# One load of a weight's first 10 KB for 128 partitions becomes loads of 5, 5, 5, 1 and 112 partitions

## The chip, the cores and the metric

The program runs on one core of a Trainium2 chip. The core has TensorE (PE, with its weight loads as PEld), VectorE (DVE), ScalarE (ACT), GpSimd (POOL) and SyncE (SP), and 16 DMA engines that move data between HBM and the on-chip memory SBUF, which has 128 partitions. The metric is the device time of one execution in microseconds; three runs are timed and the median counts. A profile of one further execution shows where the time lies.

## The reference

It is a decode step of attention with a KV cache, gated by a small MLP. All data are float32.

```
x: (2, 1, 512)   k_cache, v_cache: (2, 32, 8192, 128)   wq: (512, 4096)   wo: (4096, 512)
w1: (512, 1376)  b1: (1376)  w2: (1376, 512)  b2: (512)

xn = layernorm(x)
q  = (xn @ wq) split into 32 heads of 128
p  = softmax(q . k_cache / sqrt(128))          # one query row per head, 8192 keys
o  = p . v_cache                               # joined to (2, 1, 4096)
s  = o @ wo
g  = silu(gelu(layernorm(xn) @ w1 + b1) @ w2 + b2)
out = x + s * g
```

The caches are 537 MB together and are read once; wo is 8 MB and is read at the end.

## The kernel before

Two heads form a unit, so there are N = 32 units. Of a unit, K is 8 MB: half a head's keys stand in 64 partitions, 64 KB to a partition. Two buffers hold K in turn, a third, `big[2]`, holds V. For each unit VectorE multiplies K with the query row and sums over the 128 columns, TensorE and ScalarE do the softmax, and TensorE forms the product of the weights and V. The loops of the engines run beside each other and are tied by semaphores that are taken down again (`take`).

All big loads are issued by SP on one queue, in the order in which the code stands: w1, wq, the first K, w2, the second K, two small loads of x into `x4` (lines 299 to 301, 4 partitions with 512 B each), then V and K in turn (lines 305 to 320). ScalarE's queue carries three small loads at the very start: x (2 partitions), b1 and b2 (1 partition each; lines 199 to 201). The last V (unit 31) goes in two halves into a K buffer, so that `big[2]` is free for wo before the last unit is done.

wo is laid out as `(p c) n -> p c n`: partition p holds rows 32p to 32p+31, that is 32 pieces of 512 numbers, 64 KB. It comes in seven pieces after `p_free`, cut at c = 0, 10, 18, 24, 28, 30, 31, 32 (`WO_CUTS`, line 90), the last of them in two halves of columns (`LAST_COLS`, line 91); semaphore `d_wo0` stands for the first piece, up to `d_wo6` and `d_wol` (lines 323 to 325). The pieces shrink, so that little is left to do when the last one lands.

At the end TensorE multiplies the normalised output `on` with wo, c by c (lines 526 to 543). The first 28 go in four row groups of one bank (`pw`), ScalarE copies it (`wide`, line 378), the last four go into `acc`, and the copy is added. VectorE applies the gate and adds x (lines 379 to 381), SP stores (line 382) and waits for the store.

Each DMA raises its semaphore by 16 once it has all landed; TensorE's matmuls of a piece wait for 16 on that piece's semaphore.

## Time and profile before

| | |
|---|---|
| median of three runs | 1300.62 us (1300.08 to 1300.69) |
| the profiled execution | 1299.61 us |
| its span, first to last instruction | 1298.3 us |
| HBM read | 559.30 MB, 431 GB/s over the span |
| VectorE busy | 1135.7 us (87%) |
| TensorE busy | 460.9 us (35%) |
| ScalarE busy | 72.0 us (6%) |
| first issue of wo | 1266.90 us |
| end of TensorE's last matmul | 1295.79 us |

The span is shorter than the time of the execution by 1.31 us, which lie before the first and after the last instruction. Times in the rows are microseconds from the start of the span. The profile does not name the DMA engine that carried a packet. How many engines are at work can be read from the DMA share of a short stretch (a share of 1.00 is all 16), and how many have ended a load from the 4-byte packets, one of which closes an engine's part of a load and raises the semaphore.

### The profile page before, as it was taken

What the parts mean: (1) busy time and instruction counts of PE and PEld (TensorE: products, weight loads), DVE (VectorE), ACT (ScalarE), POOL (GpSimd) and SP (SyncE); (2) the same over time, 40 slices, a digit from 0 to 9 for tenths busy, and PEclk for the clock granted to TensorE, in tenths of its full rate; (3) what the DMA queues carried; (4) which work ended last, traced back from release to release, by engine and by line L of the source; (5) the groups of instructions that cost most, each with busy time, mean ns of one, the idle gap of its engine ahead of it and who ended that gap; (6) DMA issues with size and microseconds to landing.
All of it is one profiled execution on the core that took longest, in us unless ns stands there. A gap on an engine that the chain in (4) does not pass through costs nothing. (4 is left out here: it accounts for less than half of the span.)

```text
span 1298.3 us, 7389 instructions
## 1 busy us (share of the span) xinstructions
PE 460.9 (35%) x2958; PEld 148.7 (11%) x2958; DVE 1135.7 (87%) x171; ACT 72.0 (6%) x245; POOL 2.1 (0%) x14
## 2 busy tenths in 40 slices
PE   3813433322433322343322334322334321343337
PEld 1201111001111000111100111100111100111103
DVE  2599999988889988889988888988888988888991
ACT  1100000000000000000000000000000000000000
POOL 0000000000000000000000000000000000000000
PEclk8756776567677556777656777656776666677659
DMA  9999999999999999999999999999999999999998
GB/s 410 436 428 442 430 432 432 428 444 428 438 430 428 440 428 444 428 434 430 428 444 428 440 430 426 440 428 444 428 434 430 430 442 428 440 430 430 423 436 361
DMA packets 11242, 559.39 MB, mean 431 GB/s; under 512 B 1264, under 2 KB 1536, under 8 KB 1892
## 3 DMA queue, kind: packets, MB, share of 16 engines
q1 hardware_dynamic: 11228, 559.30, 99.7%
q8 instruction: 4, 0.07, 0.0%
q10 hardware_dynamic: 8, 0.01, 0.0%
q14 instruction: 2, 0.02, 0.0%
HBM read 559.30 MB, written 0.00 MB: 431 GB/s over the span
## 5 line engine op out<-in xcount | busy, mean ns | idle before, releaser
L51 DVE TENSOR_TENSOR big<-big,Q 128x16384 f32<-128x16384 f32 (+1 forms) x33 | 551.3, 16707 | 73.2 <-DVEq L45 73.2
L51 DVE TENSOR_REDUCE sc<-big 128x128 f32<-128x16384 f32 (+1 forms) x33 | 551.2, 16703 | 4.8
L51 PE MATMUL bank<-big,PZ 128*8 128x512 f32 x2048 | 291.1, 732 | 628.9 <-PEq L45 628.9
L51 PEld LDWEIGHTS bank<-big,PZ 128*8 128x8 f32 x2048 | 60.1, 103 | 832.6 <-issue 832.6
L51 PE MATMUL bank<-Q,ident 128*128 128x512 f32 (+2 forms) x198 | 78.5, 506 | 0.2 <-issue 0.2
L51 ACT COPY o<-bank 128x512 f32<-128x512 f32 x33 | 19.4, 586 | 891.6 <-ACTq L45 880.0
L51 PE MATMUL bank<-ident,MX 128*1 128x128 f32 x32 | 9.3, 291 | 137.9 <-PEq L45 137.8
L51 PE MATMUL bank<-mod,o 128*128 128x2 f32 x256 | 32.8, 250 | 27.4 <-PEq L45 27.4
L51 PEld LDWEIGHTS bank<-mod,o 128*128 128x128 f32 x256 | 31.0, 191 | 55.4 <-issue 55.4
L51 PEld LDWEIGHTS bank<-Q,ident 128*128 128x128 f32 x198 | 33.6, 198 | 16.5 <-issue 16.5
L51 ACT ACTIVATE PZ<-sc,bias 64x128 f32<-64x128 f32 x64 | 25.5, 399 | 6.6 <-ACTq L45 6.2
L51 DVE TENSOR_REDUCE nm<-bank 1x2 f32<-1x128 f32 x32 | 8.9, 279 | 18.9 <-DVEq L45 18.9
L51 DVE TENSOR_TENSOR big<-big,mine 64x512 f32<-64x512 f32 (+1 forms) x2 | 4.5, 2279 | 21.6 <-ACT big L51 21.6
L51 PEld LDWEIGHTS bank<-ident,MX 128*1 128x1 f32 x32 | 2.5, 79 | 162.9 <-issue 162.9
L51 ACT COPY bias<-bank 128x1 f32<-128x1 f32 x32 | 5.1, 159 | 225.2 <-ACTq L45 225.2
L51 PE MATMUL bank<-nm,srow 1*64 1x1 f32 x128 | 10.4, 219 | 10.0 <-PEq L45 9.4
L51 PE MATMUL bank<-big,sides 64*128 64x512 f32 x16 | 12.6, 958 | 3.7 <-DVE big L51 3.7
L51 DVE TENSOR_REDUCE MX<-sc 128x1 f32<-128x128 f32 x32 | 9.2, 286 | 4.7
L51 PE MATMUL bank<-big,xnT 128*2 128x512 f32 x64 | 9.3, 748 | 10.3 <-DMA big<-in_A_wq_dram 10.3
L51 ACT ACTIVATION_READ_ACCUMULATOR PZ<-sc,bias x64 | 11.8, 184 | 0.0
L51 DVE SCALAR_TENSOR_TENSOR res<-bank,gate 128x128 f32<-128x128 f32 x1 | 0.3, 292 | 12.1 <-PE bank L51 12.1
L51 PEld LDWEIGHTS bank<-nm,srow 1*64 1x64 f32 x128 | 8.6, 165 | 16.2 <-issue 16.2
(78 smaller groups left out, 74.8 us busy)
## 6 DMA issues: line engine op xcount, KB each, us to landing
big<-in_A_k_cache_dram SPq DMA_DIRECT2D x2, 4096.0 KB, 35.9
big<-in_A_v_cache_dram SPq DMA_DIRECT2D x2, 4096.0 KB, 35.9
big<-in_B_w_dram SPq DMA_DIRECT2D x1, 2752.0 KB, 10.2
big<-in_B_w_dram SPq DMA_DIRECT2D x1, 2560.0 KB, 52.1
big<-in_A_wo_dram SPq DMA_DIRECT2D x1, 2560.0 KB, 14.7
big<-in_A_wo_dram SPq DMA_DIRECT2D x1, 2048.0 KB, 19.3
big<-in_A_wo_dram SPq DMA_DIRECT2D x1, 1536.0 KB, 22.5
big<-in_A_wo_dram SPq DMA_DIRECT2D x1, 1024.0 KB, 24.5
```

Of the source, the lines that this page charges most:

```text
L51: ins = getattr(self.engines[eng], method)(*args, **kwargs)
```

## The change

The first piece of wo, c = 0 to 9 (20 KB in each partition), was one load. Its first half, c = 0 to 4 (`FEW` = 5, 10 KB in each partition), is now issued for partitions 0 to 4, 5 to 9, 10 to 14, 15 and 16 to 127 apart, in this order (`SHARES`), and its second half, c = 5 to 9, for all partitions in one load. All six loads raise `d_wo0`, so the matmuls of that piece wait for 6 x 16 = 96. The other pieces are as before.

```diff
@@ -89,6 +89,8 @@
     LAST_COLS = (0, D // 2, D)
+    FEW = 5
+    SHARES = (0, 5, 10, 15, 16, P)
@@ -320,7 +322,9 @@
     wo_v = wo.rearrange("(p c) n -> p c n", p=P)
-    for i, (c0, c1) in enumerate(zip(WO_CUTS, WO_CUTS[1:])):
+    for a0, a1 in zip(SHARES, SHARES[1:]):
+        op("SP", "dma_start", wo_sb[a0:a1, :FEW, :], wo_v[a0:a1, :FEW, :], sig="d_wo0")
+    for i, (c0, c1) in enumerate(zip((FEW,) + WO_CUTS[1:], WO_CUTS[1:])):
         for h, (n0, n1) in enumerate(zip(LAST_COLS, LAST_COLS[1:]) if c1 == OC else [(0, D)]):
@@ -525,7 +529,7 @@
-            after = [t["on"], t["mem"], (f"d_wo{i}", 16)]
+            after = [t["on"], t["mem"], (f"d_wo{i}", 16 * (len(SHARES) if i == 0 else 1))]
```

On SP, after the last two halves of V, the program's order at the loads of wo changes as follows (`big` is the buffer that wo shares with V; partitions x numbers):

```order
 L51 DMA big<-in_A_v_cache_dram 128x8192 x2
-L51 DMA big<-in_A_wo_dram 128x5120
+L51 DMA big<-in_A_wo_dram 5x2560 x3
+L51 DMA big<-in_A_wo_dram 1x2560
+L51 DMA big<-in_A_wo_dram 112x2560
+L51 DMA big<-in_A_wo_dram 128x2560
 L51 DMA big<-in_A_wo_dram 128x4096
 L51 DMA big<-in_A_wo_dram 128x3072
```

One load has become six; those behind it keep their order. On the other engines no instruction moves.

## Rows read from the trace of the kernel before

**Rows 1.** Page, parts 1 to 3: busy time, DMA share in 40 slices, packets
```profile
PE 460.9 (35%) x2958; PEld 148.7 (11%) x2958; DVE 1135.7 (87%) x171; ACT 72.0 (6%) x245; POOL 2.1 (0%) x14
...
DMA  9999999999999999999999999999999999999998
...
DMA packets 11242, 559.39 MB, mean 431 GB/s; under 512 B 1264, under 2 KB 1536, under 8 KB 1892
```

**Rows 2.** Chain that ended last, in order of time: start, length, what
```profile
1268.70 25.32 DMA big<-in_A_wo_dram
...
1294.06 1.73 PE bank L51 x40
...
1295.82 0.30 DVE res L51
```

**Rows 3.** Timeline, 1266 to 1296 us: start, length, engine, operation, idle before
```profile
1266.90 3.65 SPq L51 DMA_DIRECT2D big<-in_A_wo_dram  x8
...
1283.85 0.21 PEld L51 LDWEIGHTS bank<-big,on 128*17 128x17 f32 x8 [0.27 <-issue]
...
1292.77 0.20 PEld L51 LDWEIGHTS bank<-big,on 128*17 128x17 f32 x8 [1.48 <-DMA big<-in_A_wo_dram]
...
1295.35 0.15 PEld L51 LDWEIGHTS bank<-big,on 128*17 128x17 f32 x4 [0.17 <-DMA big<-in_A_wo_dram]
```

**Rows 4.** DMA issues: what, count, size, microseconds from issue to landing
```profile
big<-in_A_wo_dram SPq DMA_DIRECT2D x1, 2560.0 KB, 14.7
```

**Rows 5.** Stretches near the end: length, GpSimd, clock, DMA share, GB/s
```profile
1293.00:1293.20 0.20, 0.00 (x0) 1.00 1.03 369
...
1293.80:1294.40 0.60, 0.00 (x0) 1.00 0.34 121
```

**Rows 6.** Packets begun in 1273.39:1273.40 (with share), 1274.86:1275.12, 1274.91:1274.93, 1275.09:1275.12
```profile
q1 hardware_dynamic: 1, 0.00, 5.6%
...
DMA packets 13, 0.16 MB, mean 630 GB/s; under 512 B 5, under 2 KB 5, under 8 KB 5
...
DMA packets 4, 0.06 MB, mean 3072 GB/s; under 512 B 1, under 2 KB 1, under 8 KB 1
...
DMA packets 2, 0.02 MB, mean 683 GB/s; under 512 B 1, under 2 KB 1, under 8 KB 1
```

**Rows 7.** Packets begun in 73.45:73.85, 73.85:73.95 and 74.80:75.20, second K and x4
```profile
DMA packets 28, 0.53 MB, mean 1319 GB/s; under 512 B 14, under 2 KB 20, under 8 KB 20
...
DMA packets 6, 0.07 MB, mean 666 GB/s; under 512 B 3, under 2 KB 5, under 8 KB 5
...
DMA packets 8, 0.26 MB, mean 655 GB/s; under 512 B 4, under 2 KB 4, under 8 KB 4
```

**Rows 8.** ScalarE's queue: packets in 1.60:1.77 (x) and 2.75:2.76 (b1)
```profile
DMA packets 2, 0.00 MB, mean 24 GB/s; under 512 B 0, under 2 KB 0, under 8 KB 2
...
q10 hardware_dynamic: 1, 0.01, 131.9%
```

**Rows 9.** Packets begun in 1195.8:1196.36, 1196.36:1196.40 and 1197.3:1197.6
```profile
DMA packets 16, 0.52 MB, mean 936 GB/s; under 512 B 8, under 2 KB 8, under 8 KB 8
...
DMA packets 2, 0.07 MB, mean 1638 GB/s; under 512 B 1, under 2 KB 1, under 8 KB 1
...
DMA packets 8, 0.26 MB, mean 874 GB/s; under 512 B 4, under 2 KB 4, under 8 KB 4
```

**Rows 10.** Instruction queue: packets, MB, share, in 148.4:149 and 1203.60:1204.0
```profile
q14 instruction: 1, 0.01, 3.2%
...
q14 instruction: 1, 0.01, 5.1%
```

**Rows 11.** Packets begun in 1215.69:1215.79, 1216.65:1216.90 and 1216.69:1216.71
```profile
DMA packets 0, 0.00 MB, mean 0 GB/s; under 512 B 0, under 2 KB 0, under 8 KB 0
...
DMA packets 13, 0.26 MB, mean 1049 GB/s; under 512 B 5, under 2 KB 5, under 8 KB 5
...
DMA packets 2, 0.03 MB, mean 1639 GB/s; under 512 B 1, under 2 KB 1, under 8 KB 1
```

## The prediction

> **What bounds the kernel now.** Begin with the page's slices: the share of the 16 DMA engines stands at 9 tenths from the second slice to the last but one, 431 GB/s on average; VectorE, the busiest of the others, has 87% of the span [rows 1]. The kernel is bound by its loads, and each DMA engine moves 431 / 16 = 26.9 GB/s, so 10 KB of one partition (10,240 B, called a row below) cost an engine 0.38 us. Then read the chain of waits from its end: the last things on it are the wait for a piece of wo, 1.73 us of TensorE, and vector work at 1295.82 [rows 2]. The timeline of that stretch says the same from the other side: TensorE is already waiting when the later pieces arrive, 1.48 us before the fourth and 0.17 us before the last half piece [rows 3]. So whatever moves the last landing of wo moves the end by as much, 1 to 1. The first piece is different. It lands 14.7 us after its issue at 1266.90, at 1281.6, and TensorE asks for it only once the normalised attention output is there, at 1283.85 [rows 3, 4]: 2.2 us of room.

> The next view is the one that decides. Over the last microseconds the DMA share falls in steps: all engines work at 1293.0, and from 1293.8 to 1294.4 the share is 0.34, which is 5.4 of 16 [rows 5]. Eleven engines are done and five still have their last pieces to move. They are not slower, they are late: where the last load of v ends, the earliest engine writes its closing 4-byte packet at 1273.39, and five do so from 1274.86 to 1275.12, the last at about 1275.10, which is 1.71 us behind the first [rows 6]. Since all have the same bytes of wo from there on, that distance is still there at the end. An end-of-kernel gain is to be had by taking bytes from those five and from no others.

> **The change part by part.** Before, every engine carries 8 of the 128 partitions in every load. Now the first 10 KB go out as 5 + 5 + 5 + 1 rows and 112 rows. The 112 give each engine 7 rows. A load with few rows uses few engines, as the trace has it: the two 4-row loads of x late in the setup put their eight 512 B packets on engines that are among the nine earliest of the load ahead of them, none on the last four [rows 7], two packets to an engine, and the 2-row and 1-row loads of the biases and x on the other queue are 2 packets and 1 packet [rows 8]. So I take five engines, the same each time and including the four of the 4-row loads, to get one row from each 5-row load, and the first of them the single row too:
> - eleven engines: 7 rows instead of 8, -1 x 0.38 = -0.38 us;
> - four receivers: 7 + 3 = 10, +2 x 0.38 = +0.76 us;
> - the first receiver: 7 + 3 + 1 = 11, +3 x 0.38 = +1.14 us.

> [...] The 5.4 KB row of b1 left in one packet [rows 8], so the measurement decides for one engine. [...]

> So the question is whether a receiver is one of the five late ones. In the setup none of the four known receivers is: the last four engines of that load have no 512 B packet. But the latest of the four is the ninth in order: eight engines end before 73.85, then comes one that has both a 512 B pair and its own closing packet from 73.85 to 73.95 [rows 7]. An engine starts its next packet as the last one ends, so its place can be followed from load to load. I followed this one up to 1196: it is again the ninth, with eight ahead of it and four far behind, closing between 1196.36 and 1196.40 [rows 9] (meanwhile one early engine fell back, and one that stood behind has come ahead, slowly, by drift). At 1203.6 an 8 KB instruction packet of another queue arrives on one engine [rows 10]; a packet of the same kind at 148 is the one after which the early engine fell back [rows 10]. At the end of the next load the ninth place, 1215.69 to 1215.79, is empty, and the late group has five members instead of four, the new one at 1216.69 to 1216.71 [rows 11]. It lost about 1 us. By this reading the fifth late engine is a receiver. At the end of v it closes at 1274.91 to 1274.93 [rows 6], so 1274.92 - 1273.39 = 1.53 us behind the first.

> The sum, as lags behind today's first engine: the late receiver 1.53 + 0.76 = 2.29; the late engines that give, at most 1.71 - 0.38 = 1.33; an early receiver, at most 0.45 + 1.14 = 1.59 (0.45 is an estimate: 0.40 is the width of the window in which the first eight close [rows 7], and 0.05 is for drift). The last landing moves by 2.29 - 1.71 = +0.58 us.

> The other parts. Each engine now has 15 or more packets where it had 8, plus one to six closing packets; a closing packet took 5.6% of 16 engines over 0.01 us, 0.009 us [rows 6]. The extra handling of eight packets is not shown; it lies between 0 and 8 x 0.009 = 0.07 us. I take 0.04, the middle. Issues: SP's eight wo issues took 3.65 us, 0.46 each [rows 3]; there are 13 now, so +2.3 us, the last issue at about 1272.9. The cover is the v load still in flight until 1273.39 at the earliest engine [rows 6]; the first wo issue is not later, so no engine runs dry. Without that cover it would cost at most 2.3 us. SP has nothing queued behind them but the store. TensorE's wait for the first piece now asks for six loads' count instead of one and is no new instruction; with +0.6 us the piece lands at 1282.2, and the 2.2 us of room hide it. The later waits shift with the landings. Sum: 0.58 + 0.04 = +0.62 us.

> The profiled execution took 1299.61 us, of which 1298.3 are the span. By its own time the changed kernel takes 1300.23. The median of the three runs is 1.01 us above it, so the forecast on their footing is 1300.62 + 0.62 = 1301.24 us.

> **The rivals.**
> 1. Relief. No receiver is late: the instruction packet at 1203.6 falls elsewhere or not at all in the timed executions, or I lost the thread of the ninth engine between 74 and 1196 us. Then the last is the late giver at 1.33 or the first receiver at up to 1.59, and the end moves by -0.38 to -0.12, with +0.04 for packets: about 1300.4 us. For it: in the setup the four are early [rows 7]. Against it: rows 9 to 11, and the fifth receiver is known by nothing here; four of the twelve other engines are late from the start, and if it is one of those the shift is again +0.5 to +0.8. [...]
> 2. One engine for five rows. If an odd count of rows isn't dealt out one to an engine, all 16 split rows fall on one: 7 + 16 = 23 rows, +15 x 0.38 = +5.7 us on it. If it is the earliest engine the end moves by 5.7 - 1.71 = +4.0, if the latest by +5.7: about 1305.4 us, slower. It decides from the point where that engine's surplus passes 1.71 us plus 2.6, some 12 rows. For it: no odd count other than 1 stands in the trace. Against it: 1, 2 and 4 rows went to as many engines.
> 3. The split loads are dealt over all engines in equal parts. Then every engine has its old bytes, nothing moves but the packets: 1300.66 us. Rows 7 and 8 speak against it.

> **How the numbers follow.** Forecast 0.64, relief 0.24, one engine 0.04, even dealing 0.05, something not seen 0.03. What this measurement can tell from no change is about 0.2%, 2.6 us. Forecast, relief and even dealing all lie within it; one engine and half of the unseen make slower, and the rest of the unseen is divided: faster 0.02, same 0.93, slower 0.05. The range runs from the best relief, 1300.62 - 0.38, less 0.3 for the scatter of the runs (0.6 us between lowest and highest), 1299.9, to a late first receiver, 1300.62 + 0.58 + 0.38 + 0.04, plus 0.4 for scatter, 1302.1.

> **What would show it.** In the new profile: more 10 KB packets, 1 row in 16 on few engines; the DMA share after the bulk of the wo pieces standing at 1 to 3 sixteenths where it stood at five, for about 1 us; the last wo landing some 0.6 us later behind the earliest engine than 1.7 us; SP's issues at about 6 us for 13. If the late group loses 0.38 us and nothing sticks out behind it, relief is right. If one engine works alone for 4 us, rival 2 is. If the share falls as before, rival 3. The instruction packet at 1203.6 missing or on another engine would break the step that I trust least.

## The result and the profile after

The changed kernel takes 1304.71 us (median of 10 runs, 1303.81 to 1305.63), the kernel before 1300.63 (10 runs). The ratio is 1.0031 with a 95% interval of 1.0021 to 1.0041: slower by 0.3%, 4.1 us, and above the range that was given (1299.9 to 1302.1). The profiled execution took 1304.4 us with a span of 1303.1, which is 4.8 us longer than the span before.

The page of the kernel after has the same lines of busy time to within 1 us, as many bytes, and a last slice that moves 297 GB/s where it had 361. These are its DMA share, its packets and its rate [answering rows 1]:

```profile
PE 461.6 (35%) x2958; PEld 149.6 (11%) x2958; DVE 1135.7 (87%) x171; ACT 71.9 (6%) x245; POOL 2.1 (0%) x14
...
DMA  9999999999999999999999999999999999999998
...
DMA packets 11401, 559.37 MB, mean 429 GB/s; under 512 B 1296, under 2 KB 1568, under 8 KB 1924
```

The chain that ended last, kernel after, has the same members as before in [rows 2], behind more issues of SP; the wait for wo is longer, and its end has moved from 1294.02 to 1298.80, by 4.8 us:

```profile
1270.60 28.20 DMA big<-in_A_wo_dram
...
1298.85 1.75 PE bank L51 x39
...
1300.62 0.30 DVE res L51
```

The timeline of the kernel after from 1266 to 1299 us answers rows 3. Two waits are new: TensorE waits for the second half of the last V, which was there before, and for the first piece of wo, which had 2.2 us of room:

```profile
1267.06 7.32 SPq L51 DMA_DIRECT2D big<-in_A_wo_dram  x13
...
1277.50 3.62 PE L51 MATMUL bank<-big,PZ 128*8 128x512 f32 x32 [0.89 <-DMA big<-in_A_v_cache_dram]
...
1286.49 0.19 PEld L51 LDWEIGHTS bank<-big,on 128*17 128x17 f32 x8 [1.86 <-DMA big<-in_A_wo_dram]
...
1297.59 0.19 PEld L51 LDWEIGHTS bank<-big,on 128*17 128x17 f32 x8 [1.49 <-DMA big<-in_A_wo_dram]
```

Where the time went is read from one view, stretches of the timeline with the DMA share and the rate (columns: stretch, length, GpSimd busy, granted clock, DMA share, GB/s). First the kernel before:

```profile
1268.00:1273.00 5.00, 0.00 (x0) 1.00 0.99 426
1273.00:1275.00 2.00, 0.00 (x0) 1.00 0.84 358
...
1283.00:1285.00 2.00, 0.00 (x0) 1.00 0.97 414
...
1273.00:1283.00 10.00, 0.00 (x0) 1.00 0.96 410
```

And the kernel after:

```profile
1268.00:1273.00 5.00, 0.00 (x0) 1.00 1.02 439
1273.00:1275.00 2.00, 0.00 (x0) 1.00 0.86 221
...
1283.00:1285.00 2.00, 0.00 (x0) 1.00 1.01 421
...
1273.00:1283.00 10.00, 0.00 (x0) 1.00 0.96 219
```

From 1273 to 1283 us the engines are busy to the same 0.96, and move 219 GB/s instead of 410. That is (410 - 219) x 10 us = 1.91 MB less, and at 431 GB/s it takes 4.4 us to make up for them. Before 1273 and after 1283 us the rates are about equal. So for ten microseconds the engines are slow together, and none is left working alone. The tail of the kernel after has the late engines again, up to some 7 of 16 where five stood in [rows 5], for little more than a microsecond:

```profile
1298.60:1299.00 0.40, 0.00 (x0) 1.00 0.46 161
1299.00:1299.60 0.60, 0.00 (x0) 1.00 0.16 56
```

So a DMA engine counts as busy also while its packet is held up: the share is 0.96 in both, at 410 and at 219 GB/s. The share says nothing of it; the rate at the same share does.

### The profile page after: what moved, and what is told of

The parts are those of the page before. It is cut to its first block, busy times and chain, and to the rows that moved or that the text cites. A ratio compares the mean times of both kernels' runs of the same rounds, so it can differ in the third digit from the quotient of the medians.

```text
span 1303.1 us, 7394 instructions
## 1 busy us (share of the span) xinstructions
PE 461.6 (35%) x2958; PEld 149.6 (11%) x2958; DVE 1135.7 (87%) x171; ACT 71.9 (6%) x245; POOL 2.1 (0%) x14
## 2 busy tenths in 40 slices
DMA packets 11401, 559.37 MB, mean 429 GB/s; under 512 B 1296, under 2 KB 1568, under 8 KB 1924
## 5 line engine op out<-in xcount | busy, mean ns | idle before, releaser
L51 PE MATMUL bank<-big,PZ 128*8 128x512 f32 x2048 | 288.2, 726 | 629.5 <-PEq L45 628.6
L51 PE MATMUL bank<-big,on 128*17 128x512 f32 (+1 forms) x88 | 11.8, 595 | 3.9 <-DMA big<-in_A_wo_dram 3.9
```

The costliest lines, as they stand in the source:

```text
L51: ins = getattr(self.engines[eng], method)(*args, **kwargs)
```

## The experiments

Three theories stood after the result. Places, an assumption that no trace had shown: a load of 128 partitions gives each DMA engine partitions of its own, and with other counts several engines write to the same part of SBUF and hold each other up. Size or source: 10 KB pieces, or their order in HBM, are read slowly. Surplus: what the prediction had, the fullest engine sets the end. Each run is compared with the kernel before on the same chip, which took 1299.9 to 1300.0 us there. The edits shown are those at the loads; where the number of loads changes, the count that TensorE (or SP) waits for changes with it. All are against the changed kernel, but for those where half of V is cut, which are against the kernel before.

**Two halves of 10 KB, no split by partitions.**

```diff
-    SHARES = (0, 5, 10, 15, 16, P)
+    SHARES = (0, P)
```

> The first 20 KB of wo come in two loads of 10 KB, each for all 128 partitions; nothing is split by partitions. Three theories. Places: the 4 us come from splitting by partitions (a load of 128 partitions gives each DMA engine a group of partitions of its own, other counts make engines meet); here nothing meets, so 1300.6 to 1300.8 us, and 10 KB packets take 0.38 us each. Size: pieces of 10 KB out of rows of 64 KB are read more slowly than pieces of 20 KB; all 256 pieces are there as in the changed kernel, so about 1304.7 us and packets of 0.6 to 1.0 us. Surplus: the end is set by the fullest engine; here all are equal, so 1300.6 us.

1300.04 us against 1300.03, ratio 0.9999 (0.9990 to 1.0009). The stretch as above:

```profile
1273.00:1283.00 10.00, 0.00 (x0) 1.00 0.95 400
```

10 KB pieces out of rows of 64 KB run at about the old rate (400 against 410 GB/s). The theory of size falls, and the second half of the change, c = 5 to 9 in one load, costs nothing.

**The few-row loads alone.** They bring their bytes a second time, into units of Q that no one reads any more.

```diff
+    for a0, a1 in ((0, 5), (5, 10), (10, 15), (15, 16)):
+        op("SP", "dma_start", Q[a0:a1, 4:24, :]..., wo_v[a0:a1, :FEW, :]..., sig="d_few")
-    SHARES = (0, 5, 10, 15, 16, P)
+    SHARES = (0, P)
```

> As with two loads of 10 KB for all partitions, and ahead of them loads of 5, 5, 5 and 1 partitions that bring the same bytes a second time, into a part of Q that is no longer read; SP also waits for them at the end. Places: five engines at a time write into partitions 0 to 15, where two to four engines have their own data, so these meet with the last load of v and with wo: 2 to 3.7 us by a count of engines that share a group (an estimate from the 0.38 us of a row), 1302.6 to 1304.3 us. Surplus: the receivers have 3 rows more, the first 4, so at most 1.53 + 1.14 - 1.71 = +1.0 us, 1301.0 to 1301.6 us. Size: 1304.7 us or more, as for the two halves alone.

1302.04 us, ratio 1.0015 (1.0006 to 1.0025): +2.0 us, at the lower end for places. It is above the +1.0 that surplus allows, but the interval, +0.8 to +3.2 us, still holds that. What surplus does not have is the loss of rate that these 160 KB bring to the stretch:

```profile
1273.00:1283.00 10.00, 0.00 (x0) 1.00 0.97 367
```

**The load of 112 partitions alone.** The loads of 5, 5, 5 and 1 are left out.

```diff
-    for a0, a1 in zip(SHARES, SHARES[1:]):
+    for a0, a1 in ((16, P),):
```

> The loads of 5, 5, 5 and 1 partitions are left out (the first 10 KB of partitions 0 to 15 are not brought, so the products of 80 rows of wo are not right); the load of 112 partitions and the second half stay. Places: the 112 rows, 7 to an engine, lie across the groups of 8, so most engines meet another one: +1.9 to +4.8 us by the same count, 1302.5 to 1305.4 us, and the packets of 10 KB take 0.6 us and more. Surplus: every engine has a row less, so -0.4 us, 1300.2 us. Size: 240 of the 256 pieces, about 1304.3 us.

1303.63 us, ratio 1.0029 (1.0018 to 1.0041). With fewer bytes and no surplus on any engine it loses 3.6 us by the medians:

```profile
1273.00:1283.00 10.00, 0.00 (x0) 1.00 0.96 269
```

So the larger part of the cost comes with the 112 rows and not with the five-row loads. The two parts together (2.0 + 3.6) are more than the 4.1 of the whole, but by no more than the intervals of these runs, so whether they overlap is not shown.

**16 and 112 partitions.**

```diff
-    SHARES = (0, 5, 10, 15, 16, P)
+    SHARES = (0, 16, P)
```

> The first 10 KB come in one load of 16 partitions and one of 112: 1 + 7 rows for every engine, no engine has more than before. Places: still 112 rows across the groups, and 16 engines meet in the first 16 partitions: +2.6 to +6.0 us, 1303.2 to 1306.6 us. Surplus: equal bytes on every engine, so 1300.6 to 1300.8 us. Size: 1304.7 us.

1304.98 us, ratio 1.0035 (1.0021 to 1.0050), +4.95 us by the medians. If 16 and 112 rows are dealt out in equal parts, all engines have the bytes they had before, and surplus cannot make this. Here, too, the rate is what is lost:

```profile
1273.00:1283.00 10.00, 0.00 (x0) 1.00 0.94 230
```

**Another source.** The same loads to the same partitions, read from 1.3 MB without gaps.

```diff
+    wo_f = wo[:FEW * P, :].rearrange("(p c) n -> p c n", p=P)
-        op("SP", "dma_start", wo_sb[a0:a1, :FEW, :], wo_v[a0:a1, :FEW, :], sig="d_wo0")
+        op("SP", "dma_start", wo_sb[a0:a1, :FEW, :], wo_f[a0:a1], sig="d_wo0")
```

> The same five loads into the same partitions as in the changed kernel, but the rows are read from another place: row p from byte 10240 p of wo on, so 1.3 MB without gaps and not 10 KB out of every 64 KB (the numbers are not those of wo's first piece, so the product is not right). If the places in SBUF make the cost, it stays: +3.5 to +5 us over before, 1303.5 to 1305 us, with GB/s of 170 to 280 for some 7 us after the last load of v. If the way of reading HBM makes it (the order or the gaps of the rows), it goes: 1300.0 to 1300.6 us.

1304.5 us, ratio 1.0040 (1.0026 to 1.0054): the cost stays, and so does the rate:

```profile
1273.00:1283.00 10.00, 0.00 (x0) 1.00 0.94 224
```

So neither the gaps nor the addresses in HBM make it (224 GB/s here, 219 with them).

**64 and 64 partitions.**

```diff
-    SHARES = (0, 5, 10, 15, 16, P)
+    SHARES = (0, 64, P)
```

> The first 10 KB come in two loads of 64 partitions, 4 rows to each of 16 engines in both, so every engine has 8 rows as before. [...] If what counts is only that a load uses all 16 engines with equal rows: 1300.0 to 1300.5 us. If any split by partitions costs as much as that of 112 rows: +3.6 us or more.

1304.99 us, ratio 1.0039 (1.0025 to 1.0054): +5.0 us. That a balanced split costs at all speaks for places, but by its time alone this run fits the last case of the expectation, that any split by partitions costs as much as that of 112 rows. At the half rate that the long loads of 64 in the next run show (203 to 216 against 416 GB/s), the 8 rows of an engine would take 2 x 8 x 0.38 = 6.1 us instead of 3.0, an estimate of about +3.0 us, and the measured cost is more. The rate falls below half for a while:

```profile
1275.00:1277.00 2.00, 0.00 (x0) 1.00 0.77 118
1277.00:1279.00 2.00, 0.00 (x0) 1.00 0.96 241
```

Half of the 431 GB/s of the kernel before would be 215. Engines that are late with V and engines that are ahead in the next load may meet here as well; whether they do, and how much it adds, was not measured, and stays open.

**One half of V in two long loads of 64.** It asks the same of a load long enough to settle.

```diff
-        op("SP", "dma_start", KBUF[N % U][:, c0:c1], vf[N - 1][:, c0:c1], sig=f"d_v31{i}")
+        for a0, a1 in ((0, 64), (64, P)) if not i else ((0, P),):
+            op("SP", "dma_start", KBUF[N % U][a0:a1, c0:c1], vf[N - 1][a0:a1, c0:c1], sig=f"d_v31{i}")
```

> Made from the kernel before: the first 4 MB half of the last V comes in two loads of 64 partitions, 4 rows of 32 KB to an engine in each. It measures how fast a long load of 64 partitions runs, and by that how its rows are dealt. If an engine gets four neighbours (0 to 3, 4 to 7, ...), 16 engines meet two by two: 215 GB/s while it runs, +9.7 us, about 1310 us. If neighbours go to different engines (0 to engine 0, 1 to engine 1, ...), 16 engines meet four by four: 108 GB/s, up to +29 us, 1320 to 1329 us. If a load of 64 partitions were as good as one of 128: 430 GB/s and 1300 us.

1311.19 us, one run: +11.3 us.

```profile
1255.00:1260.00 5.00, 0.00 (x0) 0.50 0.99 203
1265.00:1270.00 5.00, 0.00 (x0) 1.00 1.04 216
...
1285.00:1295.00 10.00, 0.00 (x0) 0.83 0.97 416
```

At a full share the two loads run at 203 to 216 GB/s, half of the 416 of the loads of 128 behind them. That is the rate of the expectation's first case, 16 engines that meet two by two, with four neighbouring partitions to an engine; which partitions an engine got the trace does not say. +11.3 us is some more than the +9.7 that went with it.

**Eight partitions at a time, with a step of 4 and next to each other.** Both read the same rows in the same order; only the place of writing differs.

```diff
-        op("SP", "dma_start", KBUF[N % U][:, c0:c1], vf[N - 1][:, c0:c1], sig=f"d_v31{i}")
+        for r in range(16 if not i else 0):
+            src = slice(r // 4 * 32 + r % 4, r // 4 * 32 + r % 4 + 29, 4)
+            op("SP", "dma_start", KBUF[N % U][src, c0:c1], vf[N - 1][src, c0:c1], sig="d_v310")
+        if i:
+            op("SP", "dma_start", KBUF[N % U][:, c0:c1], vf[N - 1][:, c0:c1], sig="d_v311")
```

In the second, `KBUF[N % U][8 * r:8 * r + 8, c0:c1]` is written.

> Made from the kernel before: the first 4 MB half of the last V comes in 16 loads of 8 partitions, each set with a step of 4 (0, 4, ..., 28; 1, 5, ..., 29; and so on). Eight engines carry it, 16 rows of 32 KB each at 1.21 us, instead of 16 engines with 8: at least 19.4 instead of 9.7 us, so +9.7 us, and up to +19 us where the second half of these loads meets the other eight engines, which are ahead: 1310 to 1320 us. By the theory of places the sets with a step of 4 do not meet among themselves.

> The same 16 loads with the same rows read from HBM in the same order, but written to 8 partitions next to each other (0 to 7, 8 to 15, ...), so the rows of the last V stand in other partitions than they should and the last unit is not right. Engines, packets, issues and source are the same as with a step of 4; only the place in SBUF differs. Theory of places: eight engines write into two groups of four partitions, so each load runs at a quarter of the rate: +34 to +48 us over before, 1335 to 1348 us. Any theory of source, packet size or number of engines: the same time as with the step of 4, within 1 us.

1316.87 us with the step, 1354.91 next to each other, one run each; before was 1299.96. With the step +17 us, inside what was expected; side by side +55 us, more than the 34 to 48. With the step, the first eight sets go to partitions 0 to 63 and the others to 64 to 127. A stretch of each, and one in which eight engines are left:

```profile
1255.00:1260.00 5.00, 0.00 (x0) 0.52 0.98 419
...
1270.00:1275.00 5.00, 0.00 (x0) 1.00 1.01 207
...
1305.00:1310.00 5.00, 0.00 (x0) 1.00 0.49 204
```

Side by side:

```profile
1295.00:1300.00 5.00, 0.00 (x0) 0.50 0.96 114
...
1330.00:1340.00 10.00, 0.00 (x0) 0.72 0.50 212
```

In both, the eight that are left at the end have half the share and half the rate (204 and 212 GB/s at 0.49 and 0.50), so 26.0 and 26.5 GB/s each where it was 26.9 in the kernel before: nobody is held up in loads of 128 any more. In the middle sixteen engines at a full share (1.01 and 0.96) move 207 or 114 GB/s. 38 us lie between two kernels that differ in nothing but where the rows are written. That settles for these loads that the place of writing decides, against every theory of source, size, number of rows or of engines.

The step alone is not what keeps engines apart. Into partitions 0 to 63 it costs next to nothing, 419 GB/s with the other engines at work beside it; with the same step into 64 to 127 all are at half, 207 GB/s. That fits the meeting with the engines ahead that the expectation named, and with it the time passes the +9.7 us of the bytes. Which partitions share a part of SBUF was not mapped out. Nor does the plain count explain the side by side run: it has only the eight engines slowed. In the trace all are: eight engines alone move 212 GB/s at the end, and sixteen move 114. Of the 32 KB packets begun from 1254 to 1264 us none took less than 3.1 us, where they take 1.2, and from 1295 to 1300 the 20 KB packets of wo's first piece, a load of 128 partitions, took 2.5 to 3.1 us where they took 0.77 before. Why engines in loads of 128 partitions are held up by that much is open.

**The few-row loads, written with a step of 4.** The edit is against the kernel with the few-row loads alone.

```diff
-    for a0, a1 in ((0, 5), (5, 10), (10, 15), (15, 16)):
-        op("SP", "dma_start", Q[a0:a1, 4:24, :]..., wo_v[a0:a1, :FEW, :]..., sig="d_few")
+    for r, (a0, a1) in enumerate(((0, 5), (5, 10), (10, 15), (15, 16))):
+        op("SP", "dma_start", Q[r:r + 4 * (a1 - a0) - 3:4, 4:24, :]..., wo_v[a0:a1, :FEW, :]..., sig="d_few")
```

> As the kernel with two 10 KB halves and extra loads of 5, 5, 5 and 1 partitions into Q (which took 2.0 us more than before), same rows read, same engines, same bytes, but written to partitions with a step of 4 (0, 4, 8, 12, 16; then 1, 5, 9, 13, 17; then 2, 6, 10, 14, 18; then 3). If the first five engines own the groups of four from 0, 4, 8, 12 and 16 on, each of them now writes into its own group and nobody meets anyone. Places: the 10 KB packets take 0.39 us as in the two halves alone, and only the surplus is left: with a late receiver 1.53 + 1.14 - 1.71 = +1.0 us, without one +0.0 to +0.2 us; 1300.0 to 1301.0 us. If the few rows cost by their engines or by their number, not by their place: +2.0 us as before, 1302.0 us.

1300.60 us, ratio 1.0005 (0.9996 to 1.0015): +0.7 us by the medians, where the same loads next to each other cost 2.0. The intervals overlap (-0.5 to +1.9 us here, +0.8 to +3.2 us there), but the executions do not: the longest here took 1301.33 us, the shortest there 1301.56. The rate in the stretch is whole again, and TensorE's last wait, which ended at 1295.35 before [rows 3], ends 0.94 us later:

```profile
1273.00:1283.00 10.00, 0.00 (x0) 1.00 0.98 413
```

```profile
1296.29 0.16 PEld L51 LDWEIGHTS bank<-big,on 128*17 128x17 f32 x4 [0.17 <-DMA big<-in_A_wo_dram]
```

The price of a row can be read off. From 1275.3 to 1278.5 us 155 packets begin, 19 of them closing ones and 136 of 10 KB; their time is 1.035 x 16 x 3.2 us, so 0.39 us each, as expected:

```profile
DMA packets 155, 1.39 MB, mean 435 GB/s; under 512 B 19, under 2 KB 19, under 8 KB 19
...
q1 hardware_dynamic: 155, 1.39, 103.5%
```

This kernel issues 13 loads at wo and has 1296 packets under 512 B, both as the changed kernel, so it is not the number of loads or of closing packets that costs 4 us either. A kernel that writes the 112 rows to places where engines keep apart was not run: for them, the dearest part, the place of writing is what the other runs leave over.

What is left of the cost has the size of the prediction's own term: three rows more on receivers, 3 x 0.38 = 1.14, less the place of a late receiver behind the latest engine, 1.71 - 1.53 = 0.18, makes 0.96. That it comes so close to 0.94 is partly luck: the two profiles are of different executions, the medians differ by 0.67 us, and the interval holds zero. That a late engine is among the receivers can be seen, though. One of the five that are last with V writes its closing packet at 1274.79 us, and then 10 KB and a closing packet three times over, the latter at 1275.18, 1275.57 and 1275.96, which is the mark of three one-row shares. From 1274.78 to 1274.79:

```profile
DMA packets 2, 0.01 MB, mean 1024 GB/s; under 512 B 1, under 2 KB 1, under 8 KB 1
```

It is 1.37 us behind the first engine, at 1273.42, and the latest is 1.74 us behind, so the sum with the numbers of this execution is 1.37 + 1.14 - 1.74 = +0.77 us.

## Why the prediction was wrong

**What bounds the kernel.** Right. The chain after has the same members, its landing of wo moved by 4.8 us in the profiled execution and the end by the same 4.8.

**Who gets the rows, and how late they are.** The dealing of few rows to as many engines holds by the closing packets. There are 1296 packets under 512 B where there were 1264 [rows 1]: 16 for the second half, 16 for the 112 rows and 5 + 5 + 5 + 1 for the small loads, less the 16 of the one load before, make 32 more. One engine for five rows would have made 20 more, all engines for every load 80. That each of the 16 engines gets 7 of the 112 rows, as the sum has it, no run shows by itself; the runs show the 16 closing packets. The late receiver holds in the run with the step of 4, where it is seen and the end moved by 0.7 to 0.9 us. The step that was trusted least came true so far as the traces tell: an 8 KB instruction packet stands at 1203.4 to 1203.8 us in every one of them (1203.6 before, 1203.4 in the changed kernel); which engine it meets they do not say. In the changed kernel itself the surplus can't be seen apart from the rest: the split into 16 and 112, where no engine should have more than before, took no less.

**The step that failed** is the first term of the sum, "a row costs an engine 0.38 us", taken to hold for every row of every load, with "-1 x 0.38" for eleven engines. 0.38 us is what a row costs in loads of 128 partitions, the only ones of size in the trace before. From 1273 to 1283 us the changed kernel moves 219 GB/s at a share of 0.96, so a busy engine has 219 / (0.96 x 16) = 14.3 GB/s and 10 KB take it 0.72 us. The packets say the same: from 1277.6 to 1282 us, 95 of 10 KB and 15 closing ones take 0.983 x 16 x 4.4 us, 0.73 us a row:

```profile
DMA packets 110, 0.97 MB, mean 221 GB/s; under 512 B 15, under 2 KB 15, under 8 KB 15
...
q1 hardware_dynamic: 110, 0.97, 98.3%
```

By the dealing, an engine has 15 to 19 such pieces, 7 to 11 rows of the first half and 8 of the second. Loads of 128 partitions beside them are held up as well: the second half of V, for which TensorE did not have to wait before, now makes it wait 0.89 us. The 112 rows that I had counted as a relief of one row are the dearest part (+3.6 us alone). That the place of writing is behind this price is shown for few rows, by the pairs that differ in it alone; for the 112 rows it is what size, source and surplus leave over.

**The covers.** SP's 13 issues took 7.32 us, not some 6, and still cost nothing that shows, since the share stays as high through them as before (1.02 and 0.86 for 0.99 and 0.84); the cover named was the right one. The cover of TensorE's wait for the first piece, 2.2 us of room, did not do: the piece came so late that TensorE stood 1.86 us. It is not a second loss, as TensorE waits again for the pieces behind it, 1.49 us for the fourth as before. The packets' handling, 0 to 0.07 us, agrees with the two halves (0.9999), which cannot measure it. Two slips in the working change nothing: an engine has two to six closing packets, not one to six, and the upper end of the range adds up to 1302.0, not 1302.1.

**The rivals.** Relief is out. The one-engine rival had 1305.4 us, close to the measured time, and it is wrong all the same: its mark was one engine alone for 4 us at the end, and the tail has no such stretch, and the closing packets speak against it. Its small chance was given for another mechanism. Even dealing falls by the same packets. What was missing was a rival in which the place of writing sets the rate; the trace before held no large load of fewer than 128 partitions, so the price of one should have been left open far upwards rather than taken from the 128s.

## What to carry to other kernels

## What the runs showed of the hardware that had not been expected

Eight engines writing to eight neighbouring partitions pulled all transfers of the core down in the one run of it: with all 16 engines at a share of 0.96 the rate was 114 GB/s, though half of them were carrying loads of 128 partitions; with a step of 4 it was 419 while they wrote to partitions 0 to 63, and 207 in 64 to 127. Loads of 160 KB in all added 2.0 us to the kernel when side by side and 0.7 us when spread. And by the counts of the trace four engines are far behind the rest at 74 us and four are at 1197 us [rows 7, 9], which fits engines that lose time early and stay behind, though the rows do not say that they are the same; the 1.71 us by which the latest is behind at the end of V [rows 6] are paid at the end, where the share is 0.34 [rows 5].
